# Sparse attention and a gated MLP on one core: rows of q and k of the local heads loaded as twelve tokens, with a new list for the first batch

## The chip, the cores and the metric

The kernel runs on one core of a Trainium2 chip. The metric is the device time of one execution in microseconds (us), as the median of several runs.

## The reference

Eight batches of 576 tokens go through an attention of eight heads of 64 columns, whose first four heads see a window of 32 tokens (local) and whose last four see every 32nd earlier token (strided). The result, with the heads side by side, goes through a gated MLP with a spatial gate.

```python
scores = (q @ k.T) / sqrt(64)             # per batch and head, 576 x 576
local   = (rel >= 0) & (rel < 32)         # heads 0 to 3, rel = row - column
strided = (rel >= 0) & (rel % 32 == 0)    # heads 4 to 7
x = softmax(masked scores) @ v            # 576 x 512 per batch
h = gelu_tanh(x @ w_in)                   # 512 -> 1024, halves u and v
v_s = w_sg @ (layernorm(v) * g_ln) + b_sg[:, None]
out = x + (u * v_s) @ w_out
```

## The kernel before

Work is tiled by batch. A pair of heads `hh` (0 and 1 are local, 2 and 3 strided) fills 128 partitions. For each pair q and k must stand turned, with the columns of a head on partitions and tokens along the row (`qT`, `kT`). In batch 0 and for the first part of batch 1 TensorE does this: `row_load` (`LR`) brings rows of q and k, `row_turn` (`RQ`, `RK`) multiplies them with an identity into PSUM (`tqq`, `tqk`), and `row_copy` (`CQ`, `CK`) copies them out into `qT` and `kT`. From the scores (`SL` into `sa` and `sr`, `SS` into `ss`) come masks, maximum, exponent, sum and product (`MK MX SB EX SU ML`, tiles `sml` for local and `sms` for strided heads), the turned probabilities (`PL`, `PS` into `ptl`, `pts`, copied out by `CL`, `CS`), and the product with v (`VA`, `VX`, `VY` into `ol`; `PV`, `PW` into `os`). That is x, turned; it is split in a high and a low part (`XH`, `XL` into `xt`), turned once more (`XR` into `xs`) and sent to DRAM (`XD`, four DMAs from ScalarE's queue). The MLP follows: `va` to `vd` (the v half of w_in, tile `v`), `u`, the gate `s` (tile `sg`, product `gt`) and `o`.

w_in and w_out are split into two parts in the first batch's time, in 16 pieces: `cl` loads, `ca` and the alternative form of `cb` run on ScalarE (ACT), `cb`, `cc` and `cd` on VectorE (DVE), `cg` on ACT, `ch` on GpSimd (POOL) or DVE; the tiles are `stage`, `cv`, `wih` and `wil`, `cs` and `cx` for w_out. The first matmul of `v` needs pieces 0 and 1.

Nothing is scheduled by a compiler. Three lists of words are written out by hand: `START` (all of batch 0's attention, the weights, and the front part of batch 1), `CYCLE` for batches 1 to 6 and `LAST`. `emit` runs a list word by word, and each engine keeps that order, so all instructions are recorded at one line (L81) and are told apart by tile names. A word's `@n` names one of four PSUM slots, `^` takes the other engine, `-` means the batch itself and no sign the next one. SP's queue issues the loads, also in the list's order. PE runs in list order too, and a matmul that must wait holds all behind it.

For local pairs `row9_load` and `row9_turn` (from line 458) put 9 tokens of one head on each of 128 partitions and turn each token's 64x64 block by itself, 18 matmuls per tensor, each recorded as two passes; one copy of 128x576 reads the slot out. For strided pairs `row_load` and `row_turn` put 12 tokens on each of 96 partitions and turn two tokens at a time, six transposes per tensor.

Of the kernel before, what the change touches and what calls it, by code (L numbers as in the profile page):

```python
# [22 lines left out]


START = """
ml= LR-:0 RK-@1:0 LZ-:0 LR-:1 RK-@2:1 cl=:3 cb=:3 TZ-:0 CK^-:0 cl=:1 ca=:1 cb=:1 ca=:3 cc=:3 RQ-@0:0
LR-:2 TZ-:1 cd=:3 RQ-@3:1 cl=:0 CK-:1 CQ^-:1 CQ-:0 SL-@0:0 MK-:4 ca=:0 MX-:4 mk= SL-@3:1 cb^=:0
LR-:3 cc=:1 wl=:1 MK-:5 MX-:5 SB-:4 EX-:4 SB-:5 RK-@2:2 RQ-@1:2 SU-:4 CQ-:2 RK-@0:3 CK-:2 ML-:4
RQ-@3:3 CK-:3 cc=:0 EX-:5 CQ-:3 TZ:0 mp=@1 cl=:9 ca=:9 LZ-:1 SU-:5 SS-@0:2 cl=:2 SS-@3:3 PL-@1:4
CL-:4 ML-:5 cd^=:1 cg=:1 MK-:2 PL-@21:5 CL-:5 cg=:3 MK-:3 wt=@0:1 MX-:3 LR:0 CM^-:5 wb= wh=:1 TZ:1  # L30
LV-:1 VA-@2:1 LR:1 cl=:4 cd=:0 LV-:0 cg=:0 ch=:1 MX-:2 XR-:1 wm=:1 SB-:3 EX-:3 SU-:3 RK@3:1 wc=
cb=:2 CK^:1 ca=:2 cl=:5 ca=:4 RK@0:0 CK^:0 SB-:2 EX-:2 VY-@1:0 XH-:1 XL-:1 cb=:9 cl=:6 XD-:1 VX-:0
LV-:3 wd= SU-:2 we= XHa-:0 cb^=:4 ML-:3 PS-@0:3 CS-:3 cl=:8 ch=:3 RQ@3:0 ca=:6 cc=:9 XR-:0 RQ@2:1
ch^=:0 ML-:2 LV-:2 CQ^:1 CQ:0 XD-:0 PS-@3:2 cc=:4 CS-:2 cb^=:8 PV-@2:3 PW-:3 XLa-:0 va@0:0 cb^=:5
cc=:2 PV-@3:2 PW-:2 cd^=:2 cl=:11 ca=:5 vb:0 cd=:4 cb^=:6 wl=:0 XHb-:0 cc=:6 lg= XH-:2 cg=:2 ca=:8
XLb-:0 cd=:6 XL-:2 ch=:2 XR-:2 XH-:3 XL-:3 SL@1:0 cg=:6 SL@3:1 cd=:9 cg=:9 ch=:9 MK:0 vc:0 cg=:4
cl=:7 cb=:7 ca=:7 MX:0 vd:0 g:0 wt=@1:0 wh=:0 ch=:4 cc=:5 cc=:8 cc=:7 wo= wp= cd=:5 LQ:3 cd=:8 LR:2
cd=:7 wm=:0 va@3:1 XD-:2 wl=:2 vb:1 vc:1 vd:1 cg=:5 XR-:3 cl=:13 g:1 cg=:7 ch=:6 xt cl=:10 LZ:1
cg=:8 v@0:2 vh TQ:3 RK@1:2 ls:1 CK:2 vl ls:0 RQ@2:2 CQ:2 LZ:0 lm:0 wl=:4 XD-:3 g:2 ls:2 ch=:5 ch=:7
u@3:1 ug:1 lm:1 lr:2 wt=@1:2 wh=:2 cb^=:11 wm=:2 SB:0 EX:0 SU:0 u@0:0 ca=:11 ug:0 LV:0 lm:2 wl=:3  # L40
cc=:11 LV:1 ML:0 cb=:10 u@2:2 wt=@0:4 wh=:4 wm=:4 SS@3:2 MK:2 u@1:3 PL@23:0 ca=:13 ug:2 lh:0 ll:0
lh:1 ll:1 ug:3 TZ+:1 cd=:11 CL:0 wt=@0:3 wh=:3 lh:2 cl=:15 wm=:3 ll:2 MX:2 cb=:13 ca=:10 cc=:10
TZ+:0 LQ+:0 cc=:13 SS@1:3 MK:3 s@2:0 sm:0 CM^:0 VA@3:1 XR:1 SB:2 EX:2 ca=:15 cd=:10 sh:0 sl^:0 TQ+:0
cg=:10 XH:1 ch=:8 s@0:1 cl=:12 MX:3 s@2:2 LQ+:1 XD:1 SB:3 EX:3 sm:1 sh:1 SU:2 cl=:14 cd=:13 ML:2
SU:3 ML:3 XL:1 cg=:11 ch^=:11 LV:2 sm:2 sh:2 sl:2 cb^=:12 cb^=:15 s@1:3 PS@2:3 PS@3:2 ch=:10 LQ+:3
sm:3 ca=:12 sl^:1 o@0:0 o:1 cg=:13 CS:2 PV@2:2 PW:2 CS:3 cc=:15 ch=:13 ca=:14 cd=:15 cg=:15 cb=:14
cc=:14 cd^=:14 cg=:14 cc=:12 cd^=:12 cg=:12 r VA@1:0 XH:0 ch=:12 sh:3 XR:2 XD:2 mr= ch^=:14 XL:0
XH:2 ch^=:15 o@3:2 o:3 sl^:3 o2:3 LV:3 XR:0 TQ+:1 os:3 od:3 o2:2 os:2 o2:1 LQ+:2 PV@3:3 LZ+:0 PW:3
rt o2:0 XR:3 os:0 od:0 LZ+:1 XH:3 XD:0 XD:3 od:2 LV+:1 os:1 od:1 XL:2 LV+:0 XL:3
"""  # L50
# [1089 lines left out]
```

## Time and profile before

| what | value |
|---|---|
| median of 3 runs | 556.45 us (555.75 to 558.96) |
| the profiled execution, its own time | 557.88 us |
| its span, first to last instruction | 556.2 us |
| mean granted TensorE clock | 0.975 |
| busy: PE, DVE, ACT, POOL | 534.1, 395.0, 224.7, 114.3 us |
| PE share of the span | 96% |

The span is what the trace covers, and the own time has 1.7 us around it. Busy times are means over a first batch in which PE often waits and seven batches in which it hardly does.

### The profile page before, as it was taken

To read this page: it belongs to the slowest core of one execution; us is meant where nothing else is said; L and a number is where in the kernel's file an instruction comes from. 1 tells how busy PE (TensorE), PEld (TensorE's weight loads), DVE (VectorE), ACT (ScalarE), POOL (GpSimd) and SP (SyncE) were. 2 spreads that over 40 slices of the span, in tenths; PEclk is the share of its full clock that TensorE was granted. 3 is DMA by queue.
4 is the path that set the end of the run, shared out by engine and by line. 5 is a ranking of instruction groups with operands and counts; after the bars stand their busy time and mean duration, and the time that the engine had idled before them with its cause. 6 is when DMAs were issued, how large, how long until landed. Compare 5 with 4: busy or idle time off the path is not lost.

```text
span 556.2 us, 17621 instructions
## 1 busy us (share of the span) xinstructions
PE 534.1 (96%) x7667; PEld 477.4 (86%) x7667; DVE 395.0 (71%) x686; ACT 224.7 (40%) x349; POOL 114.3 (21%) x164
## 2 busy tenths in 40 slices
PE   5769999999999999999999999999999999999997
PEld 5668888888998899888998899888997889978995
DVE  1796999977956788668956779568957689454622
ACT  2474685405531255315531064415532055413420
POOL 4361713511041010301031010301031010400030
PEclk9576999999999999999999999999999999999999
DMA  8998596879717685279617585189716670045002
GB/s 233 239 233 188 143 160 107 166 155 179 156 18 175 135 126 133 38 178 166 150 17 176 98 155 139 28 181 159 156 27 143 123 173 0 30 116 146 2 1 94
DMA packets 248847, 70.12 MB, mean 126 GB/s; under 512 B 232897, under 2 KB 232897, under 8 KB 248770
## 3 DMA queue, kind: packets, MB, share of 16 engines
q1 hardware_dynamic: 167746, 50.11, 43.6%
q10 hardware_dynamic: 81024, 18.89, 16.1%
q8 instruction: 60, 0.98, 0.8%
q14 instruction: 17, 0.14, 0.1%
HBM read 50.09 MB, written 18.87 MB: 124 GB/s over the span
## 4 chain that ended last, share of the span: by engine, by line
PE 89%; DVE 4%; DMA 3%; issue 2%; ACT 1%; SPq 0%; DVEq 0%; ACTq 0%
PE v L81 19%; PE sg L81 19%; PE u L81 18%; PE o L81 17%; PE ol L81 3%; PE os L81 3%; PE sa L81 2%; PE ss L81 2%; DMA stage<-in_moe_w_in_dram 2%; PE pts L81 1%; PE tqq L81 1%; PE tqk L81 1%; PE ptl L81 1%; DMA out_dram<-ob 1%; DVE wol L81 1%
## 5 line engine op out<-in xcount | busy, mean ns | idle before, releaser
L81 PE MATMUL sg<-wsh,vg 128*128 128x288 f32 x512 | 107.9, 296 | 0.1
L81 PE MATMUL u<-xt,wih 128*128 128x288 f32 x512 | 102.4, 295 | 0.0
L81 PE MATMUL o<-woh,vg 128*128 128x512 f32 x288 | 95.0, 397 | 0.6 <-ACT pts L81 0.6
L81 PE MATMUL v<-wih,xt 128*128 128x512 f32 x256 | 84.6, 400 | 0.0
L81 PEld LDWEIGHTS sg<-wsh,vg 128*128 128x128 f32 x512 | 83.6, 188 | 0.9 <-ACT ptl L81 0.3
L81 PEld LDWEIGHTS u<-xt,wih 128*128 128x128 f32 x512 | 82.3, 188 | 0.9 <-issue 0.3
L81 PE MATMUL sg<-wsl,vg 128*128 128x288 f32 x256 | 75.5, 295 | 0.3 <-DVE wsl L81 0.3
L81 PE MATMUL u<-xt,wil 128*128 128x288 f32 x256 | 75.5, 295 | 0.0
L81 PEld LDWEIGHTS o<-woh,vg 128*128 128x128 f32 x288 | 54.1, 188 | 13.1 <-ACT pts L81 1.7
L81 ACT ACT_TABLE_LOAD x30 | 38.5, 1283 | 55.4 <-DMA xd<-xs 21.2
L81 DVE TENSOR_TENSOR gt<-sg,u 128x576 f32<-128x576 f32 x32 | 23.6, 753 | 51.8 <-PE sg L81 37.8
L81 PEld LDWEIGHTS v<-wih,xt 128*128 128x128 f32 x256 | 48.6, 190 | 10.9
L81 PE MATMUL o<-wol,vg 128*128 128x512 f32 x144 | 56.2, 390 | 0.0
L81 PE MATMUL v<-wil,xt 128*128 128x512 f32 x128 | 50.4, 394 | 0.0
L81 POOL TENSOR_TENSOR vg<-gt,vg 128x576 fp32r<-128x576 f32 (+2 forms) x36 | 35.6, 1012 | 71.5 <-ACT vg L81 71.5
L81 PEld LDWEIGHTS sg<-wsl,vg 128*128 128x128 f32 x256 | 48.0, 188 | 0.6 <-DVE wsl L81 0.6
L81 PEld LDWEIGHTS u<-xt,wil 128*128 128x128 f32 x256 | 48.0, 188 | 0.0
L81 DVE TENSOR_TENSOR ob<-o,xn 128x512 f32<-128x512 f32 x32 | 21.6, 677 | 28.2 <-PE o L81 28.1
L81 POOL TENSOR_TENSOR sms<-sms,mx 100x576 f32<-100x576 f32 x10 | 12.5, 1258 | 140.4 <-DVE mx L81 140.3
L81 DVE BATCH_NORM_STATS2 bnst<-hv 128x6 f32<-128x512 f32 (+1 forms) x40 | 26.9, 672 | 13.5 <-ACT hv L81 13.5
L81 ACT CAST vg<-gt 128x576 fp32r<-128x576 f32 (+2 forms) x48 | 22.3, 512 | 32.3 <-DVE gt L81 32.3
L81 ACT COPY pts<-pts 100x576 f32<-100x576 f32 x16 | 10.1, 638 | 54.2 <-PE pts L81 27.5
(140 smaller groups left out, 922.7 us busy)
## 6 DMA issues: line engine op xcount, KB each, us to landing
xd<-xs ACTq DMA_DIRECT2D x128, 72.0 KB
xn<-xd SPq DMA_DIRECT2D x8, 1024.0 KB
out_dram<-ob ACTq DMA_DIRECT2D x32, 256.0 KB
rawq<-in_q_dram SPq DMA_DIRECT2D x100, 72.0 KB
rawk<-in_k_dram SPq DMA_DIRECT2D x100, 72.0 KB
v<-in_v_dram SPq DMA_DIRECT2D x16, 288.0 KB
...
```

Of the source, the lines that this page charges most:

```text
L81: ins = self.tc.keep_in_program_order(op(*args, **kwargs))
```

## The change

`row9_load` and `row9_turn` go. All four pairs take the form with 12 tokens on 96 partitions and six transposes. For a local pair the tokens of a head then stand in the wrong half of the partitions for every second token, so `row_copy` reads a slot out in four quarters of 64 partitions x 288; two of them read from one half of the partitions and write into the other. It concerns eight tensors (q and k of two local pairs, batches 0 and 1): PE's passes for them go from 288 to 48, the copies from 8 to 32. `START` is written anew throughout, the loads' order included; `CYCLE` and `LAST` stay.

```diff
--- before.py
+++ after.py
@@ -23,30 +23,30 @@
 START = """
-ml= LR-:0 RK-@1:0 LZ-:0 LR-:1 RK-@2:1 cl=:3 cb=:3 TZ-:0 CK^-:0 cl=:1 ca=:1 cb=:1 ca=:3 cc=:3 RQ-@0:0
-LR-:2 TZ-:1 cd=:3 RQ-@3:1 cl=:0 CK-:1 CQ^-:1 CQ-:0 SL-@0:0 MK-:4 ca=:0 MX-:4 mk= SL-@3:1 cb^=:0
-LR-:3 cc=:1 wl=:1 MK-:5 MX-:5 SB-:4 EX-:4 SB-:5 RK-@2:2 RQ-@1:2 SU-:4 CQ-:2 RK-@0:3 CK-:2 ML-:4
-RQ-@3:3 CK-:3 cc=:0 EX-:5 CQ-:3 TZ:0 mp=@1 cl=:9 ca=:9 LZ-:1 SU-:5 SS-@0:2 cl=:2 SS-@3:3 PL-@1:4
-CL-:4 ML-:5 cd^=:1 cg=:1 MK-:2 PL-@21:5 CL-:5 cg=:3 MK-:3 wt=@0:1 MX-:3 LR:0 CM^-:5 wb= wh=:1 TZ:1
-LV-:1 VA-@2:1 LR:1 cl=:4 cd=:0 LV-:0 cg=:0 ch=:1 MX-:2 XR-:1 wm=:1 SB-:3 EX-:3 SU-:3 RK@3:1 wc=
-cb=:2 CK^:1 ca=:2 cl=:5 ca=:4 RK@0:0 CK^:0 SB-:2 EX-:2 VY-@1:0 XH-:1 XL-:1 cb=:9 cl=:6 XD-:1 VX-:0
-LV-:3 wd= SU-:2 we= XHa-:0 cb^=:4 ML-:3 PS-@0:3 CS-:3 cl=:8 ch=:3 RQ@3:0 ca=:6 cc=:9 XR-:0 RQ@2:1
-ch^=:0 ML-:2 LV-:2 CQ^:1 CQ:0 XD-:0 PS-@3:2 cc=:4 CS-:2 cb^=:8 PV-@2:3 PW-:3 XLa-:0 va@0:0 cb^=:5
...
+LR-:0 RQ-@2:0 RK-@0:0 cl=:1 LR-:1 RQ-@1:1 ca=:1 LR-:2 CQ^-:0 TZ-:0 CQ-:1 CK^-:0 cl=:3 ml= SL-@0:0
+MK-:4 MX-:4 SB^-:4 ca=:3 cb^=:1 cb^=:3 TZ-:1 cc=:1 cl=:0 RK-@2:1 LZ-:1 CK-:1 ca=:0 cb=:0 cd^=:1
+cc=:3 cd^=:3 cg=:3 SL-@1:1 MK-:5 MX-:5 RK-@2:2 CK-:2 LZ-:0 wl=:1 EX-:4 LR-:3 RK-@1:3 cc=:0 SU-:4
+RQ-@0:2 wb= mk= mp=@2 CK-:3 cl=:9 LV-:1 CQ-:2 SS-@0:2 MK-:2 SB-:5 RQ-@1:3 CQ^-:3 cg=:1 SS-@1:3 LV-:0
+TZ:1 LR:0 wc= ML-:4 EX-:5 PL-@3:4 CL-:4 wt=@2:1 wh=:1 SU-:5 ML-:5 PL-@30:5 MK-:3 MX-:3 MX-:2 wm=:1
+CL-:5 CM-:5 VA-@2:1 SB-:3 EX-:3 SU-:3 SB-:2 EX-:2 TZ:0 wd= cd^=:0 ML-:3 cl=:2 ca=:2 cb^=:2 LR:1
+ca=:9 XH-:1 RK@1:0 RQ@1:0 CK:0 XL-:1 XR-:1 XD-:1 ch=:3 cl=:4 RK@0:1 we= CK:1 VY-@3:0 ca=:4 SU-:2
+VX-:0 RQ@1:1 cb=:4 cl=:6 ca=:6 XHa-:0 CQ^:0 cl=:8 ca=:8 cc=:2 cd^=:2 PS-@0:3 CQ:1 cc=:4 LV-:3 ML^-:2
+cg=:0 cl=:5 PS-@1:2 XLa-:0 CS-:3 ch=:1 PV-@2:3 PW-:3 XR-:0 ch^=:0 cb=:6 cc=:6 cb=:8 CS-:2 cc=:8
+cd=:8 XD-:0 cb=:9 LV-:2 cd=:4 cd=:6 cg=:4 cc=:9 va@0:0 vb:0 cb=:5 cg=:2 wl=:0 PV-@3:2 PW-:2 cl=:7
...
@@ -453,42 +453,8 @@
     ROWS = S // RT
     HOMES = ("wsh", "wsl", "wol", "woh")
 
-    ROWS9 = S // 9
-
-    def row9_load(b, hh):
-
-        if b == 0:
-            both = p1.tile([P, 2, 9 * D], F32, tag=HOMES[hh], name=f"rows_{b}_{hh}")
-        for n, (nm, src) in enumerate((("q", q), ("k", k))):
-            if b == 0:
-                raw = both[:, n]
-            else:
-                raw = p1.tile([P, 9 * D], F32, tag="raw", name=f"rows{nm}_{b}_{hh}", bufs=4)
-            sp.dma_start(
-                raw, src[b, 2 * hh : 2 * hh + 2].rearrange("h (p j) d -> (h p) (j d)", j=9)
-            )
-            state[b, hh, "raw" + nm] = raw
-
-    def row9_turn(b, hh, nm):
-
-        raw = state[b, hh, "raw" + nm]
-        ps = psum(f"tq{nm}_{b}_{hh}").rearrange("p a c -> p (a c)")
-        state[b, hh, "rows"] = True
-        state[b, hh, "turn" + nm] = ps[:, 0:S].rearrange("p (j m) -> p m j", m=ROWS9)
-        for j in range(9):
-            for hp in range(2):
-                r = slice(ROWS9 * hp, ROWS9 * hp + ROWS9)
-                pe.matmul(
-                    ps[64 * hp : 64 * hp + 64, j * ROWS9 : j * ROWS9 + ROWS9],
-                    raw[r, j * D : j * D + D], ident[r, r],
-                    start=True, stop=True,
-                )
-
     def row_load(b, hh):
 
-        if hh < NH // 2:
-            row9_load(b, hh)
-            return
         if b == 0:
             both = p1.tile([P, 2, 2 * RT * D], F32, tag=HOMES[hh], name=f"rows_{b}_{hh}")
         for n, (nm, src) in enumerate((("q", q), ("k", k))):
@@ -504,13 +470,10 @@
 
     def row_turn(b, hh, nm):
 
-        if hh < NH // 2:
-            row9_turn(b, hh, nm)
-            return
         raw = state[b, hh, "raw" + nm]
         ps = psum(f"tq{nm}_{b}_{hh}")
         state[b, hh, "rows"] = True
-        state[b, hh, "turn" + nm] = ps[:, :, 0:SH].rearrange("p a (c m) -> p m a c", m=ROWS)
+        state[b, hh, "turn" + nm] = ps[:, :, 0:SH]
         for j in range(RT):
             half, col = divmod(j, RT // 2)
             pe.transpose(
@@ -527,13 +490,22 @@
             state[b, hh, nm] = p2.tile([P, S + ST], F32, tag=nm + "T", name=f"{nm}T_{b}_{hh}")
             dst = state[b, hh, nm][:, 0:S]
         if hh < NH // 2:
-            to = dst.rearrange("p (m j) -> p m j", j=9)
+            to = dst.rearrange("p (m a c t) -> p t m a c", a=2, c=RT // 2, t=2)
+            of = src.rearrange("p a (c h m) -> p h m a c", h=2, m=ROWS // 2)
+            parts = [
+                (to[64 * h : 64 * h + 64, t], of[64 * t : 64 * t + 64, h])
+                for h in range(2) for t in range(2)
+            ]
         else:
-            to = dst.rearrange("p (m a c) -> p m a c", a=2, c=RT // 2)
-        if alt[0]:
-            dve.tensor_copy(to, src)
-        else:
-            act.copy(to, src)
+            parts = [(
+                dst.rearrange("p (m a c) -> p m a c", a=2, c=RT // 2),
+                src.rearrange("p a (c m) -> p m a c", m=ROWS),
+            )]
+        for to, of in parts:
+            if alt[0]:
+                dve.tensor_copy(to, of)
+            else:
+                act.copy(to, of)
 
     def k_zeros(b, hh):
 
```

PE at the start of the program (`tqq`, `tqk` are turned rows, `sa` and `sr` local scores). Before:

```order
L81 MATMUL tqk_0_124<-ident,rows_0_121 64x64 x18
L81 MATMUL tqk_1_148<-ident,rows_1_145 64x64 x18
L81 MATMUL tqq_0_179<-ident,rows_0_121 64x64 x18
L81 MATMUL tqq_1_204<-ident,rows_1_145 64x64 x18
L81 MATMUL sa_229<-kT_0_169,qT_0_227 32x64 x36
L81 MATMUL sa_229<-kT_1_201,qT_1_225 32x64 x22
L81 MATMUL sr_285<-kT_1_201,qT_1_225 32x64 x2
L81 MATMUL sa_229<-kT_1_201,qT_1_225 32x64 x6
L81 MATMUL sr_285<-kT_1_201,qT_1_225 32x64 x6
```

The same place on PE in the changed kernel:

```order
L81 MATMUL tqq_0_96<-ident,rows_0_93 128x96 x6
L81 MATMUL tqk_0_103<-ident,rows_0_93 128x96 x6
L81 MATMUL tqq_1_114<-ident,rows_1_111 128x96 x6
L81 MATMUL sa_171<-kT_0_131,qT_0_126 32x64 x36
L81 MATMUL tqk_1_221<-ident,rows_1_111 128x96 x6
L81 MATMUL sa_171<-kT_1_217,qT_1_133 32x64 x22
L81 MATMUL sr_241<-kT_1_217,qT_1_133 32x64 x2
L81 MATMUL sa_171<-kT_1_217,qT_1_133 32x64 x6
L81 MATMUL sr_241<-kT_1_217,qT_1_133 32x64 x6
```

The first scores now stand between the third and the fourth turned tensor, and the rows come q first.

ACT, the part that turns batch 1's local rows while batch 0's probabilities `pts` are copied out. Before:

```order
L81 ACTIVATE sms_90<-sms_90 100x16x36
L81 CAST xt<-ol_1_525 128x2x9x32
L81 DMA xd_645<-xs_1_576 32x18x32 x4
L81 CAST wst<-bst 32x576
L81 CAST xt<-ol_0_636 128x2x8x32
L81 ACTIVATE stage<-stage 128x512
L81 COPY pts_3_711<-pts_3_694 100x576
L81 ACTIVATE cv_735<-stage 128x512
L81 COPY qT_0_766<-tqq_0_716 128x576
L81 DMA xd_645<-xs_0_738 32x18x32 x4
L81 COPY pts_2_790<-pts_2_772 100x576
```

On ACT, from the split of `ol_1` to the copy of `pts_3`, in the changed kernel:

```order
L81 ACTIVATE cx<-cs_338 128x256
L81 CAST xt<-ol_1_494 128x2x9x32
L81 COPY kT_0_539<-tqk_0_555 64x288 x4
L81 DMA xd_576<-xs_1_574 32x18x32 x4
L81 COPY kT_1_429<-tqk_1_583 64x288 x4
L81 ACTIVATE cv_600<-stage 128x512
L81 ACTIVATE cv_647<-stage 128x512
L81 CAST xt<-ol_0_595 128x2x8x32
L81 ACTIVATE cx<-cs_655 128x256
L81 COPY qT_1_677<-tqq_1_638 64x288 x4
L81 CAST wih<-cv_234 128x512
L81 COPY pts_3_707<-pts_3_660 100x576
```

Three sets of quarters for batch 1 now stand on ACT ahead of the copy of `pts_3`, with four DMA issues between the first two; before, no copy for batch 1 stood ahead of it.

DVE, the same part. Before:

```order
L81 TENSOR_SCALAR stage<-stage 128x512
L81 COPY kT_1_519<-tqk_1_587 128x576
L81 COPY kT_0_379<-tqk_0_614 128x576
L81 TENSOR_TENSOR xt<-ol_1_525,xt 128x2x9x32
L81 TENSOR_SCALAR cs_384<-cs_384 128x256
L81 TENSOR_REDUCE sr_2_686<-sms_90 100x16
```

On DVE, from the sums of `sms_90` on, in the changed kernel:

```order
L81 TENSOR_REDUCE sr_2_602<-sms_90 100x16
L81 TENSOR_SCALAR sr_2_602<-sr_2_602 100x16
L81 RECIPROCAL sr_2_602<-sr_2_602 100x16
L81 TENSOR_SCALAR stage<-stage 128x512
L81 COPY qT_0_650<-tqq_0_562 64x288 x4
L81 SCALAR_TENSOR_TENSOR cv_545<-cv_545,stage 128x512
L81 SCALAR_TENSOR_TENSOR cv_545<-stage,cv_545 128x512
L81 SCALAR_TENSOR_TENSOR cv_600<-cv_600,stage 128x512
L81 TENSOR_TENSOR sms_90<-sms_90,sr_2_602 100x16x36
L81 TENSOR_TENSOR xt<-ol_0_595,xt 128x2x8x32
```

Of batch 1's local copies DVE keeps `qT_0` alone, and takes the product on `sms_90` from POOL.

## Rows read from the trace of the kernel before

**Rows 1.** The chain of waits that ended last: start us, us, what.

```profile
38.16 4.12 issue
```

**Rows 2.** Stretches: window, length, busy us (instructions) of PE, PEld, DVE, ACT, POOL; PEclk, DMA, GB/s.

```profile
5.00:10.00 5.00, 3.66 (x68) 3.47 (x67) 0.00 (x0) 0.00 (x0) 2.82 (x11) 1.00 0.94 283
10.00:15.00 5.00, 3.53 (x79) 3.39 (x76) 2.09 (x4) 1.83 (x4) 0.00 (x0) 1.00 1.04 227
...
42.30:50.00 7.70, 7.68 (x130) 6.78 (x130) 4.57 (x8) 3.42 (x7) 0.00 (x0) 0.50 0.83 196
50.00:80.00 30.00, 30.00 (x444) 25.97 (x443) 27.86 (x55) 21.98 (x39) 13.70 (x15) 1.00 0.81 157
```

**Rows 3.** Timeline of PE: start us, us, operation, count [idle before, releaser].

```profile
18.67 0.77 PE L81 MATMUL sa<-kT,qT 64*32 64x64 f32 x35 [0.62 <-issue]
...
20.11 1.22 PE L81 MATMUL tqk<-ident,rows 96*128 96x96 f32 x6
21.13 1.16 PE L81 MATMUL tqq<-ident,rows 96*128 96x96 f32 x6
...
24.71 2.54 PE L81 MATMUL ss<-kT,qT 64*36 64x36 f32 x128
...
42.28 2.61 PE L81 MATMUL tqq<-ident,rowsq 64*64 64x64 f32 x44 [4.12 <-issue]
...
45.75 1.94 PE L81 MATMUL os<-pts,v 36*64 36x36 f32 x64
47.62 0.79 PE L81 MATMUL v<-wih,xt 128*128 128x512 f32 x1
...
51.44 0.50 PE L81 MATMUL v<-wih,xt 128*128 128x512 f32 x1
...
53.03 1.42 PE L81 MATMUL sa<-kT,qT 64*32 64x64 f32 x116
```

**Rows 4.** Waits of PE from 47.6 us on: us in total, times, longest.

```profile
PE ptl L81 <- DVE sms L81: 1.2, 1, 1.2
PE pts L81 <- DVE gt L81: 0.9, 1, 0.9
```

**Rows 5.** Groups of PE up to 50 us, by form: count, busy us, mean ns, idle before.

```profile
L81 PE MATMUL tqq<-ident,rowsq 64*64 64x64 f32 x72 | 3.6, 278 | 4.1 <-issue 4.1
...
L81 PE MATMUL tqk<-ident,rows 96*128 96x96 f32 x12 | 2.4, 369 | 0.0
```

**Rows 6.** DMA of 39 to 41 us: queue, packets, MB, share of 16 engines.

```profile
q8 instruction: 1, 0.02, 2.9%
```

**Rows 7.** Timeline of ACT: start us, us, operation, count [idle before, releaser].

```profile
13.16 1.24 ACT L81 ACTIVATE cv<-stage 128x512 f32<-128x512 f32 x2 [8.84 <-DMA stage<-in_moe_w_in_dram]
...
14.83 0.62 ACT L81 COPY qT<-tqq 128x576 f32<-128x576 f32 x1
17.98 0.67 ACT L81 ACTIVATE cv<-stage 128x512 f32<-128x512 f32 x1 [2.53 <-DMA stage<-in_moe_w_in_dram]
...
46.09 0.64 ACT L81 COPY pts<-pts 100x576 f32<-100x576 f32 x1 [2.43 <-DMA xd<-xs]
...
52.64 0.44 ACT L81 ACTIVATE cx<-cs 128x256 f32<-128x256 f32 x1
52.97 0.63 ACT L81 CAST xt<-os 128x576 fp32r<-128x576 f32 x1
...
62.22 0.62 ACT L81 CAST wih<-cv 128x512 fp32r<-128x512 f32 x1 [1.43 <-DMA xd<-xs]
```

**Rows 8.** Timeline of DVE, same columns.

```profile
10.88 0.43 DVE L81 TENSOR_SCALAR stage<-stage 128x512 int32<-128x512 int32 x1 [10.88 <-DMA stage<-in_moe_w_in_dram]
...
26.66 3.07 DVE L81 TENSOR_TENSOR sms<-ss,mask_s 36x576 f32<-36x576 f32 x4
...
44.94 0.76 DVE L81 COPY qT<-tqq 128x576 f32<-128x576 f32 x1 [3.11 <-PE tqq L81]
```

**Rows 9.** Page, costliest groups: count, busy us, mean ns, idle before.

```profile
L81 POOL TENSOR_TENSOR sms<-sms,mx 100x576 f32<-100x576 f32 x10 | 12.5, 1258 | 140.4 <-DVE mx L81 140.3
```

More of the change, by code (lines that the diff above doesn't have):

```diff
@@ L31 @@
-LV-:1 VA-@2:1 LR:1 cl=:4 cd=:0 LV-:0 cg=:0 ch=:1 MX-:2 XR-:1 wm=:1 SB-:3 EX-:3 SU-:3 RK@3:1 wc=
-cb=:2 CK^:1 ca=:2 cl=:5 ca=:4 RK@0:0 CK^:0 SB-:2 EX-:2 VY-@1:0 XH-:1 XL-:1 cb=:9 cl=:6 XD-:1 VX-:0
-LV-:3 wd= SU-:2 we= XHa-:0 cb^=:4 ML-:3 PS-@0:3 CS-:3 cl=:8 ch=:3 RQ@3:0 ca=:6 cc=:9 XR-:0 RQ@2:1
-ch^=:0 ML-:2 LV-:2 CQ^:1 CQ:0 XD-:0 PS-@3:2 cc=:4 CS-:2 cb^=:8 PV-@2:3 PW-:3 XLa-:0 va@0:0 cb^=:5
-cc=:2 PV-@3:2 PW-:2 cd^=:2 cl=:11 ca=:5 vb:0 cd=:4 cb^=:6 wl=:0 XHb-:0 cc=:6 lg= XH-:2 cg=:2 ca=:8
-XLb-:0 cd=:6 XL-:2 ch=:2 XR-:2 XH-:3 XL-:3 SL@1:0 cg=:6 SL@3:1 cd=:9 cg=:9 ch=:9 MK:0 vc:0 cg=:4
@@ L37 @@
[L37 to L48, printed above, removed]
@@ L49 @@
-rt o2:0 XR:3 os:0 od:0 LZ+:1 XH:3 XD:0 XD:3 od:2 LV+:1 os:1 od:1 XL:2 LV+:0 XL:3
+LR-:0 RQ-@2:0 RK-@0:0 cl=:1 LR-:1 RQ-@1:1 ca=:1 LR-:2 CQ^-:0 TZ-:0 CQ-:1 CK^-:0 cl=:3 ml= SL-@0:0
[3 more added lines that the diff above has]
+TZ:1 LR:0 wc= ML-:4 EX-:5 PL-@3:4 CL-:4 wt=@2:1 wh=:1 SU-:5 ML-:5 PL-@30:5 MK-:3 MX-:3 MX-:2 wm=:1
@@ new lines @@
+CL-:5 CM-:5 VA-@2:1 SB-:3 EX-:3 SU-:3 SB-:2 EX-:2 TZ:0 wd= cd^=:0 ML-:3 cl=:2 ca=:2 cb^=:2 LR:1
[3 more added lines that the diff above has]
+cd=:8 XD-:0 cb=:9 LV-:2 cd=:4 cd=:6 cg=:4 cc=:9 va@0:0 vb:0 cb=:5 cg=:2 wl=:0 PV-@3:2 PW-:2 cl=:7
+ch=:2 ch=:4 cd^=:9 cg=:9 ch=:9 SL@1:0 XHb-:0 XLb-:0 SL@3:1 XR-:2 cl=:11 cb=:11 XH-:2 XH-:3 XL-:2
@@ new lines @@
+vc:0 cb=:7 ca=:7 cc=:7 ca=:5 cc=:5 XL-:3 vd:0 g:0 LR:2 xt MK:0 LQ:3 cd^=:7 cg=:7 ch=:7 LZ:1 wo=
+va@1:1 vb:1 cg=:6 MX:0 XD-:2 ch=:6 wt=@0:0 TQ:3 cl=:13 lg= wh=:0 wm=:0 vc:1 vd:1 g:1 cd=:5 wp= cg=:5
+ch=:5 wl=:2 cl=:10 v@0:2 ls:1 XR-:3 ca=:11 RK@3:2 CK:2 u@1:1 vh XD-:3 vl g:2 cl=:15 ls:0 lm:0
+wt=@2:2 wh=:2 ls:2 wm=:2 SB:0 EX:0 ug:1 RQ@3:2 u@0:0 ug:0 lm:1 lr:2 u@2:2 CQ:2 SU:0 lh:1 SS@3:2
+cc=:11 ug:2 lm:2 ll:1 ML:0 wl=:4 LV:1 wt=@1:4 wh=:4 MK:2 u@2:3 SS@0:3 PL@21:0 wm=:4 MX:2 wl=:3 LZ:0
+LV:0 lh:2 lh:0 ll:0 ug:3 cb^=:13 ll:2 wt=@3:3 CL:0 ca=:13 cc=:13 wh=:3 wm=:3 TZ+:1 LQ+:0 SB:2 LQ+:1
@@ new lines @@
+EX:2 cd^=:11 cg=:11 MK:3 ch^=:11 cb=:10 MX:3 s@2:0 CM^:0 cd^=:13 ca=:10 VA@3:1 s@0:1 LV:2 sm:0 sh:0
+cc=:10 cd^=:10 cb=:15 cg=:13 XR:1 cg=:10 ca=:15 cc=:15 XH:1 cl=:14 XD:1 SB:3 TZ+:0 TQ+:0 sl^:0
+cl=:12 sm:1 sh:1 SU:2 XL:1 ch=:10 cg=:8 sl^:1 EX:3 SU:3 s@1:2 cb=:14 sm:2 ML^:2 s@0:3 sm:3 LQ+:3
+ca=:12 ML:3 PS@2:3 cb^=:12 sh:2 ch=:13 rt VA@3:0 PS@1:2 CS:3 ca=:14 ch^=:8 cc=:12 o@0:0 o:1 LV:3
+cc=:14 o@2:2 cd=:12 XH:0 sl:2 cd=:14 CS:2 PV@1:2 PW:2 cg=:12 cd=:15 cg=:15 o:3 TQ+:1 ch^=:15 sh:3
+mr= ch=:12 XR:2 r XL:0 cg=:14 ch^=:14 sl^:3 o2:2 XR:0 o2:3 os:3 XD:2 os:2 od:2 LQ+:2 LZ+:0 XH:2
@@ L50 @@
+PV@3:3 PW:3 XH:3 XL:2 o2:1 o2:0 os:1 XR:3 XL:3 os:0 XD:3 XD:0 LZ+:1 od:0 LV+:1 od:1 od:3 LV+:0
 """
```

## The prediction

> **What bounds the kernel now.** I read the chain of waits that ended last first. Nearly all of it is PE's own matmuls; the one long piece of it that is neither work nor the first loads is 4.12 us at 38.16 us, an idle PE with nothing to wait for [rows 1]. The stretches come next: from 50 to 80 us PE is busy for all 30.00 us, so from the first `v` matmul on PE sets the end, and a change in the first 50 us is worth what it moves that start [rows 2]. In the timeline of PE that start is at 47.62 us, right behind `os`, and the 4.12 us stand ahead of batch 1's last turned rows [rows 3]. Not all of a shift at 47.62 us reaches the end: later PE waits 1.2 us and 0.9 us for DVE, and a PE that comes later waits less there [rows 4]. The working below is a walk from the loads to `os`. Its sum is made against the profiled execution's own 557.88 us, which is 1.43 us above the median of 556.45 us. About 0.5%, or 2.8 us, is what a measurement here can tell from no change: faster is below 553.7 us, slower above 559.2 us.
>
> **Passes.** 240 of 288 passes on PE go. 72 old passes (two tensors) took 3.6 us, 12 new ones (two tensors) 2.4 us [rows 5], and start to start six new ones take 1.0 us [rows 3]. Batch 1's four tensors so cost 4 us in place of 7. Batch 0's lie in waits for loads, where they are worth nothing as such.
>
> **The idle 4.12 us.** It ends with no event of another engine; within 39 to 41 us one packet of 0.02 MB for instructions landed on queue q8 [rows 6]. I read it as PE waiting for its own instructions, after long runs of passes of a few tens of ns each. With 240 fewer in front of it, it most likely goes. [...]
>
> What is late next, once the stall is gone, is ACT. So I walk through its new order.
>
> **Loads.** `cl3` is now the eighth load, 2752 KB through its end by the tile sizes. Before, 1664 KB had landed at 10.88 [rows 8], 2176 KB at 13.16 and 3264 KB at 17.98 us [rows 7], and between the last two 2752 KB falls at 15.7. All six row loads before it now have 96 rows in place of 128. The stretch with 128-row loads moved 283 GB/s, the next 227 [rows 2], so a load of 288 KB could take 1.30 in place of 1.04 us, and four more of this kind are 1.0 us. I take the middle, 16.2 (15.7 to 16.7).
>
> **A quarter copy.** The trace has no copy of 64 x 288, and none from one half of the partitions to the other. From below: 256 columns on ACT go by in 0.33 us, start to start (52.64 to 52.97); from above: a whole copy of 576 takes 0.62 [rows 7]. 288 columns are nearest to the first: I take 0.35, so 1.4 us for a set of four, against 0.6 for the copy that it replaces.
>
> **The walk.** ACT operations over 512 or 576 columns are 0.6 us [rows 7], DVE's 0.75 [rows 8].
> - `cl3` 16.2; ACT does one `cv`, two stage tails and the set of `kT_1`, 0.6 + 1.2 + 1.4: 19.4. Then the second local scores, 1.4 (before: 18.67 to 20.11 [rows 3]): 20.8. So nothing is won in the first 20 us, though the first scores come sooner.
> - `tqk_2`, `tqk_3`, `tqq_2`: 3 x 1.0, 23.8. ACT's copy of `qT_2` 0.6, `ss_2` half of 2.54 us [rows 3]: 25.7. DVE: two masks of 0.77 [rows 8] and `qT_3` 0.8: 28.0. `ss_3` 1.3: 29.3. Both `ss` ended at 27.2 before.
> - DVE masks `sms_91` 1.5 and takes its maximum: 31.5. POOL subtracts in `sms_91` and `sms_90`, 1.26 each [rows 9]: 34.1. ACT's exponent of the second: 34.7.
> - ACT then has `wst`, `cv`, a tail, `cx` and the high part of `ol_1`, 4 x 0.6 + 0.3: 37.4. Set `kT_0`: 38.8. Four DMA issues of `xd`: ACT stood still 2.43 and 1.43 us at two such sets [rows 7]; the middle, 1.9: 40.7. Set `kT_1`: 42.1. Two `cv`, the high part of `ol_0`, `cx`, 2.1: 44.2. Set `qT_1`: 45.6. `wih` and the copy of `pts_3`, 1.2: 46.8.
> - `os_3` 1.9 [rows 3]: **`v` starts at 48.7**, against 47.62: 1.1 later. DVE's own set, `qT_0`, ends near 42 and its product on `sms_90` near 44, hidden under ACT's work; were ACT 3 us shorter they would be next. SP brings batch 1's rows behind two sets of v loads now; I cost that at nothing, since `tqk_0` isn't wanted before 37.4 us, and what they came later than that would be late in full. POOL has two products fewer.
>
> **The clock.** [...] Six `v` matmuls took 2.75 us at the lower level and six 1.59 us at the upper (51.44 to 53.03) [rows 3]. The new list puts twelve of them ahead of `os_2`, behind a PE that waits for ACT much of the time. If the clock again rises about 8 us after steady work resumes (here `os_3` at 46.8), all twelve run at the lower level: 1.2 us more. PE is then 2.3 us behind.
>
> **What is absorbed.** Between batch 1's first local mask and its third `gt`, the new DVE order has two `cv` words (0.7 each), a stage tail and one small `cx` fewer, some 1.9 us. DVE then comes no later than before, and the 2.1 us that PE waited for it [rows 4] can swallow nearly all of the lag: 0.2 is left. If DVE gains nothing, 2.3 are left. I take 1.0. **Sum:** 557.88 + 1.0 = 558.9 for such an execution, and 556.45 + 1.0 = **557.5 for the median**.
>
> **Rivals.**
> - *Faster: ACT keeps up.* `cl3` at 15.7 (0.5), DMA issues that run beside copies (1.9), POOL's two subtractions beside other work (1.3) and quarters at 0.33 take some 4 us from the walk: `v` starts near 44.5, the stall's 4.12 us and the passes are won. 3.2 us earlier than before, with DVE's 1.9 us to keep it: 553.3. For it: the engine's queue runs ahead of its work elsewhere. Against it: 2.43 us is what such an issue cost at just this place.
> - *Slower: quarters cost as much as whole copies.* If reading across partition halves or the short rows make one quarter 0.6 us, the four sets on ACT are 4 x 4 x 0.27 = 4.3 us longer, all on the walk. The lag is 6.6, less 2.1 absorbed: 4.5, 560.9. It turns the sign from about 0.5 us a quarter on. Against it: the 256-column rows.
> - *Loads of 96 rows take a third longer.* Their 288 KB then need 1.39 in place of 1.04 us, 1.4 us by `cl3`, 0.9 more than the walk has: 558.4. Against it: 512 KB without such loads took 2.28 us (10.88 to 13.16) and 1088 KB with two of them 4.82, the same 225 KB a us. [...]
> - *The stall comes back behind `v`'s start.* The 64 passes of `os`, 72 records of scores and 128 of `ss` are still there. 4.1 us once more, less 2.1 absorbed: 560.8. That the change does less than it says is part of this: the passes go, the stall stays.
>
> **How the numbers follow.** Forecast 0.45, with a range of its own of 555 to 560; ACT keeps up 0.24; quarters dear 0.15; loads slower 0.08; stall again 0.08. Faster: 0.22 of the first rival and 0.03 of the forecast, 0.25. Slower: 0.13, 0.03 and 0.07 of the others and 0.05 of the forecast, 0.28. The rest, 0.47, is within 0.5%. The range goes from a little below the first rival, 552.8, to a little above the second, 561.3.
>
> **What would show it.** Right: no idle piece of some us put down to "issue" on PE before `v`; ACT busy without a gap from about 35 to 47 us; PE ahead of `os_3` waiting for ACT's copy of `pts_3`; first `v` at 48 to 49.5; quarters of 0.3 to 0.45; waits of PE for DVE behind 50 us well under 2.1. Wrong: a first `v` before 46, quarters over 0.5 us, `cl3` outside 15 to 17, or an "issue" idle of several us behind `v`'s start. Behind 104 us nothing should differ by more than some tenths.

## The result, and the profile after

The changed kernel takes 561.64 us (median of 8 runs, 560.18 to 563.29), the kernel before 555.84 us in its 8 runs of the same comparison (555.14 to 558.96). The ratio is 1.0089, 95% interval 1.0062 to 1.0116: slower by 3.4 to 6.4 us, clear of noise. The forecast was 557.5 with "within 0.5%" as the likeliest class; the time lies 0.3 us above the range's upper end, and in the class "slower", which had 0.28. Beside three experiments the unchanged copy of the changed kernel came out at 1.0083 (1.0057 to 1.0110).

The profiled executions differ by less, 561.47 against 557.88 us, since that of before lies 2 us above the median of its runs and that of after on it. So the traces have 3.6 us to explain.

The chain that ended last, after: two of the quarter copies on it, the first `v`, and the first scores of `CYCLE` (start, us, what). A word in small letters means the batch itself, so `CYCLE`'s first pass does the MLP of batch 1 and the scores of batch 2.

```profile
36.05 0.42 ACT kT L81
...
40.45 0.42 ACT kT L81
...
48.42 5.11 PE v L81 x12
...
125.47 1.30 PE sa L81 x82
```

The same chain of before, two runs of turning passes on it, and the same scores:

```profile
31.75 2.63 PE tqk L81 x60
...
42.28 2.61 PE tqq L81 x44
...
121.73 1.31 PE sa L81 x84
```

The 4.12 us of [rows 1] are not in this trace; the longest piece of the chain put down to "issue" ahead of the first `v` is 0.39 us now (39.63). But `CYCLE`'s first scores come 3.74 us later (125.47 against 121.73); from there on both kernels run the same lists, and the span ends 3.6 us later (559.8 against 556.2). So all of it is made in `START`. The path to the first `v` has changed: before, the passes that turn batch 1's local rows lay on it and none of their copies; now three sets of quarter copies on ACT do, and none of the passes. PE after (start, us, operation, count, idle before and releaser), which answers to [rows 3]:

```profile
31.57 1.72 PE L81 MATMUL ol<-ptl,v 64*64 64x32 f32 x56 [1.86 <-issue]
...
37.37 1.22 PE L81 MATMUL tqq<-ident,rowsq 96*128 96x96 f32 x6 [2.50 <-ACT kT L81]
...
45.17 0.90 PE L81 MATMUL pts<-ident,sms 36*100 36x36 f32 x16 [1.56 <-ACT qT L81]
46.48 1.94 PE L81 MATMUL os<-pts,v 36*64 36x36 f32 x64 [0.40 <-ACT pts L81]
48.35 0.79 PE L81 MATMUL v<-wih,xt 128*128 128x512 f32 x1
...
53.46 1.14 PE L81 MATMUL os<-pts,v 36*64 36x36 f32 x64
54.53 1.41 PE L81 MATMUL sa<-kT,qT 64*32 64x64 f32 x116
57.06 0.25 PE L81 MATMUL sr<-kT,qT 64*32 64x64 f32 x2 [1.12 <-DVE xt L81]
...
57.56 0.50 PE L81 MATMUL v<-wih,xt 128*128 128x512 f32 x1
```

The first `v` starts at 48.35 (47.62 before), so 0.7 us late; the first `sa` behind it at 54.53 (53.03), 1.5 late; the second half of `v` at 57.56. ACT, which answers to [rows 7]:

```profile
13.41 0.66 ACT L81 ACTIVATE cv<-stage 128x512 f32<-128x512 f32 x1 [1.11 <-DMA stage<-in_moe_w_in_dram]
...
35.63 1.68 ACT L81 COPY kT<-tqk 64x288 f32<-64x288 f32 x4
37.24 2.05 ACTq L81 DMA_DIRECT2D xd<-xs  x4
39.58 1.72 ACT L81 COPY kT<-tqk 64x288 f32<-64x288 f32 x4 [2.27 <-DMA xd<-xs]
...
43.45 1.67 ACT L81 COPY qT<-tqq 64x288 f32<-64x288 f32 x4
...
45.78 0.64 ACT L81 COPY pts<-pts 100x576 f32<-100x576 f32 x1
```

ACT is busy from 34 to 46.4 us but for 2.27 us at the four DMA issues, and `os` waits for its copy of `pts`. A quarter takes 0.42 us, a set 1.7. DVE:

```profile
31.20 0.27 DVE L81 TENSOR_TENSOR wst<-wsgT,wsh 64x128 fp32r<-64x128 f32 x1
...
39.45 1.85 DVE L81 COPY qT<-tqq 64x288 f32<-64x288 f32 x4
```

A set on DVE takes 1.85. The 1.86 us at 31.57 that the timeline of PE puts down to "issue" are DVE's: `ol` takes the PSUM slot that the first of these rows (`wst`, until 31.47) still reads, and every trace of the new list has the piece there, 1.85 to 1.89 us long. PE's waits from 46 to 127.2 us (total, times, longest), which answer to [rows 4]:

```profile
PE sr L81 <- DVE xt L81: 1.1, 1, 1.1
PE sg L81 <- ACT ptl L81: 0.9, 1, 0.9
PE sg L81 <- DVE wsl L81: 0.8, 1, 0.8
PE u L81 <- POOL wil L81: 0.7, 1, 0.7
PE ptl L81 <- ACT u L81: 0.5, 1, 0.5
PE os L81 <- ACT pts L81: 0.4, 1, 0.4
```

That is 4.4 us, where before had 2.4 in this stretch. Neither of the two waits that were to shrink is there; five new ones are, and the one of `sg` for `wsl` has grown from 0.3 to 0.8.

The granted clock after, in the stretches around the first `v` (length, PE's busy time and instructions, PEclk, DMA, GB/s):

```profile
46.00:50.00 4.00, 3.60 (x70) 0.50 0.87 205
50.00:52.00 2.00, 2.00 (x6) 0.50 0.57 145
52.00:54.00 2.00, 2.00 (x41) 0.74 0.72 221
54.00:56.00 2.00, 1.94 (x159) 1.00 1.19 202
```

The same of before:

```profile
50.00:52.00 2.00, 2.00 (x68) 0.95 0.94 246
```

The upper level comes some 3 us later.

### The profile page after: what moved, and what is told of

Same layout as the page of the kernel before. It is cut to its first block, busy times and chain, and to the rows that moved or that the text cites. A ratio compares the mean times of both kernels' runs of the same rounds, so it can differ in the third digit from the quotient of the medians.

```text
span 559.8 us, 17173 instructions
## 1 busy us (share of the span) xinstructions
PE 531.4 (95%) x7427; PEld 473.5 (85%) x7427; DVE 397.7 (71%) x702; ACT 229.8 (41%) x361; POOL 111.4 (20%) x160
## 3 DMA queue, kind: packets, MB, share of 16 engines
q10 hardware_dynamic: 81024, 18.89, 16.2%
HBM read 50.09 MB, written 18.87 MB: 123 GB/s over the span
## 4 chain that ended last, share of the span: by engine, by line
PE 89%; ACT 3%; DMA 2%; DVE 2%; SPq 1%; issue 1%; POOL 1%; ACTq 0%
PE sg L81 21%; PE v L81 19%; PE o L81 18%; PE u L81 18%; PE os L81 3%; PE ol L81 3%; PE ss L81 2%; PE sa L81 2%; DMA stage<-in_moe_w_in_dram 2%; PE pts L81 1%; SPq L81 1%; ACT kT L81 1%; PE ptl L81 1%; DVE sms L81 1%; PE sr L81 0%
## 5 line engine op out<-in xcount | busy, mean ns | idle before, releaser
L81 POOL TENSOR_TENSOR vg<-gt,vg 128x576 fp32r<-128x576 f32 (+2 forms) x36 | 35.7, 1013 | 74.6 <-ACT vg L81 74.1
```

The lines of the kernel that those rows point to most:

```text
L81: ins = self.tc.keep_in_program_order(op(*args, **kwargs))
```

## The experiments

**Form and list apart.** Two kernels take one half of the change each. e1, against the changed kernel (the list is that of before throughout):

```diff
-LR-:0 RQ-@2:0 RK-@0:0 cl=:1 LR-:1 RQ-@1:1 ca=:1 LR-:2 CQ^-:0 TZ-:0 CQ-:1 CK^-:0 cl=:3 ml= SL-@0:0
+ml= LR-:0 RK-@1:0 LZ-:0 LR-:1 RK-@2:1 cl=:3 cb=:3 TZ-:0 CK^-:0 cl=:1 ca=:1 cb=:1 ca=:3 cc=:3 RQ-@0:0
...
```

e2, against it (the three functions are those of before):

```diff
+        if hh < NH // 2:
+            row9_load(b, hh)
+            return
...
-            to = dst.rearrange("p (m a c t) -> p t m a c", a=2, c=RT // 2, t=2)
+            to = dst.rearrange("p (m j) -> p m j", j=9)
...
```

> The list of before with the twelve-token form and the quarter copies. Theory (the new list loses the time, not the form): 240 passes are gone, and with them the idle 4.12 us; against that six quarter sets on DVE and ACT take 1.1 us more each, partly under other work. First v matmul at 44 to 47 us, median 552 to 556 us, faster than before or the same. Rival (the form loses it: quarter copies of 0.42 us and loads of 96 rows): first v at 48 or later, median 559 us or more.

> The new list with nine tokens on 128 rows, 64x64 passes and one copy per tensor, as before. Theory (the list loses it): still slower than before, 559 to 564 us; each copy on ACT is 1.1 us shorter but 240 passes are back, and PE waits for ACT and DVE in the same places; first v at 47 to 50 us. Rival (the form loses it): 557 us or less, first v at 46 or earlier.

e1: 1.0038 (1.0004 to 1.0072), 559.71 against 556.79 us. e2: 1.0046 (1.0009 to 1.0083), 559.04. By their middles each half costs about half of the loss, and together they make the 1.0089. Both theories put it all on the list: in e1 the rival came out instead (first `v` behind 48, above 559 us), in e2 the theory, at its lower edge. So neither half alone is to blame. In e1 the first `v` came at 49.97, 2.4 us later than before, and from there to `CYCLE`'s first scores all took as long as before. Its PE still stood idle with nothing to wait for that the trace shows, 2.00 us, now in another place, between the transposes of one tile of `w_sg`:

```profile
29.35 0.46 PE L81 MATMUL wsgT<-ident,wsg 64*128 64x64 f32 x8
31.81 0.24 PE L81 MATMUL wsgT<-ident,wsg 64*64 64x64 f32 x2 [2.00 <-issue]
```

So dropping 240 passes doesn't remove such an idle piece for certain. Where the form lost its time here DVE shows:

```profile
37.00 3.73 DVE L81 COPY kT<-tqk 64x288 f32<-64x288 f32 x8
...
46.15 1.85 DVE L81 COPY qT<-tqq 64x288 f32<-64x288 f32 x4
```

The eight quarters lie on e1's chain, 3.6 us where two whole copies take 1.5. The other set ends at 48.00, and `os`, which takes the slot that it reads, starts at 48.10; the 2.43 us that the profile puts down to "issue" ahead of `os` are this set (before, the one copy ended at 45.70 [rows 8] and `os` started at 45.75). In e2 the first `v` came at 46.85, sooner than before, but `sr` waited 1.51 us, 1.02 us ahead of `sa` were put down to "issue", the granted clock fell once more (0.63 and 0.51 from 56 to 60 us), and `CYCLE`'s first scores came at 126.0.

**What the quarters cost.** e5 reads each local tensor out in two copies over all 128 partitions. It leaves out the crossing of the halves, so only its time is of use.

```diff
-            parts = [
-                (to[64 * h : 64 * h + 64, t], of[64 * t : 64 * t + 64, h])
-                for h in range(2) for t in range(2)
-            ]
+            parts = [(to[:, t], of[:, t]) for t in range(2)]
```

> The changed kernel with each local tensor read out by two copies of 128 x 288 in place of four of 64 x 288; nothing crosses the partition halves, so tokens of the local heads stand in wrong places. It halves the copy time and keeps all else. Theory (the form's cost is its copies: four sets of 1.7 us on ACT and two of 1.87 us on DVE stand on the way to the first v): a set takes 0.85 to 0.95 us, the first v comes 2 to 3.5 us before that of the changed kernel run beside it, and 1.5 to 3 us of the time come back. Rival (the copies lie under other waits): the time within 1 us of the changed kernel.

1.0028 (1.0003 to 1.0054), 558.13 against the 560.83 of e8 beside it: 2.7 us back. Its ACT and its PE:

```profile
41.70 0.73 ACT L81 COPY qT<-tqq 128x288 f32<-128x288 f32 x2
```

```profile
45.53 0.79 PE L81 MATMUL v<-wih,xt 128*128 128x512 f32 x1
```

Two copies take 0.72 us where four took 1.70, and the first `v` is at 45.53, against 49.18 in e8. The theory held: the copy sets stand in the way of the first `v`. Its sets were a little shorter than expected (0.85 to 0.95) and the first `v` 3.65 us sooner, not 2 to 3.5.

**A third form.** e10 (list of before) and e11 (new list) load six tokens of both heads per row, turn each token of each head by itself into its own half of the partitions, and read out with one copy.

```diff
+                    heads.rearrange("h (p j) d -> p h (j d)", j=RT),
...
+                    pe.matmul(
+                        ps[64 * hp : 64 * hp + 64, half, col * ROWS : col * ROWS + ROWS],
+                        raw[:, (hp * RT + j) * D : (hp * RT + j + 1) * D], ident[0:ROWS, 0:ROWS],
```

> The list of before with a third form: 96 rows hold six tokens of both heads, each token of each head is turned by a matmul of 96 x 64 into its own half of the partitions (12 matmuls, 24 passes per tensor in place of 36), and one copy of 128 x 576 reads the slot out. 96 passes fewer than before, no copy more. Theory (passes and code are worth something, quarters cost): 0 to 4 us faster than before, first v at 43.5 to 47.6. Rival (the idle PE put down to instructions comes back in another place, and loads of 96 rows in 1536-byte pieces are slower): as before or up to 3 us slower.

> The same third form with the new list. Theory (the quarters cost the form's share of the loss, the list the rest): copies on ACT and DVE are 0.64 and 0.75 us again, first v 2 to 4 us sooner than in the changed kernel, 557 to 560 us, that is 0.1 to 0.5% over before. Rival (the quarters were not what cost): within 1 us of the changed kernel.

e10: 1.0041 (1.0007 to 1.0074); its profiled execution was a short one (span 554.0), but its runs scatter from 554.99 to 563.09, and its trace has 2.77 us of "issue" in the middle of a set of scores. e11: 1.0097 (1.0067 to 1.0127), no gain over the changed kernel, against the theory; its first `v` came at 49.93, later than the changed kernel's 48.35. Its PE:

```profile
34.21 0.31 PE L81 MATMUL ol<-ptl,v 64*64 64x32 f32 x1 [2.41 <-issue]
...
37.96 2.19 PE L81 MATMUL tqq<-ident,rowsq 96*64 96x96 f32 x24 [0.79 <-ACT kT L81]
39.94 2.13 PE L81 MATMUL tqk<-ident,rowsk 96*64 96x96 f32 x24
```

One tensor's 24 passes take 2.0 us start to start (37.96 to 39.94), where six took 1.0. In e11 the copies are short again, and the chain runs through the passes of all four tensors and an idle 2.41 us in the middle of `ol`. A tensor's passes and its copies take 1.0 and 1.7 us in the changed kernel, 1.8 and 0.62 before [rows 5, 7], 2.0 and 0.64 in e11, 1.0 and 0.72 in e5. They are not to be added up as they stand, since only a part of each lies on the path: in e11 the passes and the idle piece, in the changed kernel the copies. Without the 2.41 us e11's first `v` would come at some 47.5 (an estimate from these rows), about where it was before; so it is not shown that the third form itself loses.

**What follows the first `v`.** e3 puts `os_2` between the two sixes of `v`, as before; e4 splits `os_2` before it is turned.

```diff
-cd=:8 XD-:0 cb=:9 LV-:2 cd=:4 cd=:6 cg=:4 cc=:9 va@0:0 vb:0 cb=:5 cg=:2 wl=:0 PV-@3:2 PW-:2 cl=:7
+cd=:8 XD-:0 cb=:9 LV-:2 cd=:4 cd=:6 cg=:4 cc=:9 va@0:0 cb=:5 cg=:2 wl=:0 PV-@3:2 PW-:2 vb:0 cl=:7
```

```diff
-ch=:2 ch=:4 cd^=:9 cg=:9 ch=:9 SL@1:0 XHb-:0 XLb-:0 SL@3:1 XR-:2 cl=:11 cb=:11 XH-:2 XH-:3 XL-:2
+ch=:2 ch=:4 cd^=:9 cg=:9 ch=:9 SL@1:0 XHb-:0 XLb-:0 SL@3:1 cl=:11 cb=:11 XH-:2 XH-:3 XL-:2 XR-:2
```

> The changed kernel with os_2 behind the first six v matmuls, as in the list of before, in place of behind twelve. Theory (a lag of 1.2 us comes from twelve matmuls at the lower clock, and 1.1 us of PE waiting at sr comes from os_2 being late for its readers): the wait at sr shrinks to 0 to 0.3 us, the second half of v starts 1 to 1.5 us earlier than 57.56, and 1 to 2 us of the time come back (559.5 to 560.5). Rival (later waits for ACT, DVE and POOL set the end anyway): within 0.5 us of the changed kernel.

> The changed kernel with one word moved: the turning of os_2 into xs comes behind its split in high and low part, as before, so that ACT's read of os_2 does not wait for DVE's. Theory: ACT's split starts 0.8 us earlier, the 1.12 us of waiting at sr go, 0.5 to 1.1 us of the time come back. Rival (absorbed later): no difference, within 0.4 us.

e3: 1.0090 (1.0051 to 1.0128), e4: 1.0082 (1.0045 to 1.0119). With intervals of 2 us either way these times can't tell the theories from the rival, but the traces can: what was to come back did not. In e3 the wait at `sr` was gone, but `os_2` now waited 0.67 us for DVE's split of `ol_0`, whose slot it takes. Its matmuls also stayed slow for longer, and the second half of `v` came at 60.31:

```profile
57.69 2.03 PE L81 MATMUL sa<-kT,qT 64*32 64x64 f32 x115
```

These scores took 1.41 us in the changed kernel, and e3's `os_2` 1.94 in place of 1.14, as long as `os_3` took in the changed kernel (46.48) at a granted clock of 0.50. (e3's profile gives the granted clock as 1.00 throughout; the matmuls' own times contradict it.) In e4 ACT's split starts right behind `os_2`, and `sr` still waited 0.99 us, now for the turning: `sr` takes `os_2`'s slot, whose three readers (ACT's 0.6 us, DVE's 0.76 and 0.77) run one behind the other in either order.

**ACT ahead of the first `v`.** e6, e9 and e12 move the copy of `pts_3` and `wih` ahead of the set of `qT_1`, and turn `pts_2` behind six `v`; they differ in where the DMA issues stand.

```diff
...
-PS-@0:3 CQ:1 cc=:4 LV-:3 ML^-:2
-cg=:0 cl=:5 PS-@1:2 XLa-:0 CS-:3 ch=:1 PV-@2:3 PW-:3 XR-:0 ch^=:0 cb=:6 cc=:6 cb=:8 CS-:2 cc=:8
+PS-@0:3 CS-:3 cg=:0 CQ:1 cc=:4 LV-:3 ML^-:2
+cl=:5 PV-@2:3 PW-:3 XLa-:0 ch=:1 XR-:0 ch^=:0 va@0:0 XHb-:0 XLb-:0 XD-:0 PS-@1:2 cb=:6 cc=:6 cb=:8 CS-:2 cc=:8
...
```

(This is e12; e6 has both `XD` behind `CS-:2` and `XHb` behind them, e9 `XD-:1` behind `cg=:0` and `XD-:0` behind `CS-:2`. e12 also splits `os_2` before it is turned, as e4 does.)

> The changed kernel with ACT's order changed ahead of the first v: the four DMA issues of ol_1's rows come behind the copy of pts_2, the copy of pts_3 and the wih that v needs come ahead of the set of qT_1, and pts_2 is turned between the first and second six v matmuls. Theory (ACT's order sets the first v): the first v at 45 to 46.5, 2 to 3 us sooner; of this 1 to 3 us reach the end, 558 to 560. Rival (what follows the first v, the readers of os_2 and later waits, sets the end): the first v sooner, but the time within 1 us of the changed kernel.

> The ACT order of e6_pts_first mended: ol_1's four DMA issues stand behind the copy of pts_3 and ahead of the set of qT_1, and the last 64 columns of ol_0 are split ahead of the second four issues, not behind them. Theory (where ACT's DMA issues stand cost e6 its 10 us): first v 2 to 3 us sooner than in the changed kernel, os_2 waits under 1 us, the time 1 to 3 us under the changed kernel. Rival (any delay of the weights' conversion on ACT costs the same): os_2 or the second half of v waits again, the time as in the changed kernel or above.

> As e9_act_order, but ol_1's four DMA issues stay where the changed kernel has them, ol_0's stand ahead of the copy of pts_2, and os_2 is split before it is turned. Theory (e9's 3.88 us at sr came from late sends, which hold SP's loads of v_2 and the buffer of xs_2, not from the copies' order): first v near 46.2 us as in e9, v_2 loaded in time, the wait at sr 1.2 us or less, the second half of v 1 to 2.5 us sooner than 57.6, 558 to 560 us. Rival (the new list's loss lies behind the first v whatever ACT does): sr waits 2 us or more again, or the time stays at 561 and above.

In all three the first `v` came where it was expected, 45.5, 46.4 and 46.5, and in none did the time come back: 1.0254 (1.0218 to 1.0290), 1.0168 (1.0144 to 1.0192) and 1.0102 (1.0054 to 1.0149). In e6 eight DMA issues in one piece held ACT, with the last 64 columns of `ol_0` behind them (ACT's queue), and `os_2`, which takes `ol_0`'s slot, waited 5.37 us:

```profile
48.89 4.93 ACTq L81 DMA_DIRECT2D xd<-xs  x8
53.86 1.14 ACT L81 CAST wih<-cv 128x512 fp32r<-128x512 f32 x2 [4.39 <-DMA v<-in_v_dram]
...
55.21 0.20 ACT L81 CAST xt<-ol 128x64 fp32r<-128x64 f32 x1
```

In e9 ol_1's sends went out later, and with them SP's loads of `v_2` (49.57, SP's queue; 41.99 in e12) and the turning of `os_2` (57.15, DVE); `sr` waited 3.88 us. In e12, which mends these and turns `os_2` later, `sr` waited 0.36, and yet:

```profile
44.66 1.94 PE L81 MATMUL os<-pts,v 36*64 36x36 f32 x64 [0.74 <-ACT pts L81]
46.52 0.79 PE L81 MATMUL v<-wih,xt 128*128 128x512 f32 x1
...
53.08 1.94 PE L81 MATMUL os<-pts,v 36*64 36x36 f32 x64
54.95 2.04 PE L81 MATMUL sa<-kT,qT 64*32 64x64 f32 x116
57.34 0.32 PE L81 MATMUL sr<-kT,qT 64*32 64x64 f32 x2 [0.36 <-DVE xs L81]
...
58.17 0.61 PE L81 MATMUL v<-wih,xt 128*128 128x512 f32 x1
```

The first `v` is 1.8 us sooner than in the changed kernel, the second half 0.6 later (58.17). Every piece between takes longer: `os` 1.94 us against 1.14 at 53.46 in the changed kernel, `sa` 2.04 against 1.41. The clock of e12:

```profile
50.00:52.00 2.00, 2.00 (x12) 0.50 0.31 50
...
54.00:56.00 2.00, 2.00 (x114) 0.50 1.17 225
...
58.00:60.00 2.00, 2.00 (x14) 0.89 0.51 70
```

It stays at the lower level to about 58 us. What PE did before was much the same in both, with 0.74 us of idle time ahead of `os` here; why the level rose 5 us later here was not settled. In e9, whose PE goes through the same list and the same 0.74 us up to there, the second six `v` already ran at the upper level from 49.75 on (0.39 us for a `wil` matmul, against 0.63 in e12). So e12's trace doesn't show what its order of ACT is worth with the clock of the others.

**The first set on ACT.** e7 moves the set of `kT_1` for batch 0 ahead of the words that wait for `cl3`.

```diff
-MK-:4 MX-:4 SB^-:4 ca=:3 cb^=:1 cb^=:3 TZ-:1 cc=:1 cl=:0 RK-@2:1 LZ-:1 CK-:1 ca=:0
+TZ-:1 RK-@2:1 CK-:1 MK-:4 MX-:4 SB^-:4 ca=:3 cb^=:1 cb^=:3 cc=:1 cl=:0 LZ-:1 ca=:0
```

> The changed kernel with the set of kT_1 for batch 0 ahead of the weight words that wait for the second load of w_in on ACT. Theory (the walk on ACT and DVE hands a gain on): the second local scores start 2 to 3 us sooner than at 16.1, the strided scores 1 to 2 us, the first v 0.5 to 1.5 us. Rival (the conversion of weights, now later, is what v waits for, or other waits fill in): the first v not sooner, the time within 1 us.

> The changed kernel once more, beside these three: 0.6 to 1.2% slower than before.

1.0085 (1.0058 to 1.0112) against e8's 1.0083 (1.0057 to 1.0110). The second scores came at 14.40, 2.6 us sooner than in e8, and two tensors later PE waited for rows instead; the first `v` was no sooner (49.75 against 49.18):

```profile
20.89 1.19 PE L81 MATMUL tqk<-ident,rows 96*128 96x96 f32 x6 [2.91 <-DMA rows<-in_k_dram]
```

No version here beats the kernel before.

## Why the prediction was right and wrong

**Right: the walk's end.** The first `v` was forecast at 48.7 and came at 48.35, with ACT the engine that sets it and `os_3` waiting for the copy of `pts_3`, as said. Step by step:

| milestone, us | forecast | measured |
|---|---|---|
| `cl3` landed | 16.2 | 13.4 |
| second local scores done | 20.8 | 18.5 |
| both `ss` done | 29.3 | 27.5 |
| high part of `ol_1` done | 37.4 | 35.7 |
| set `kT_0` done | 38.8 | 37.3 |
| DMA issues past | 40.7 | 39.6 |
| set `kT_1` done | 42.1 | 41.3 |
| set `qT_1` done | 45.6 | 45.1 |
| first `v` | 48.7 | 48.35 |

That it came within 0.35 us is in part luck: two sizes were off and partly made up for each other, the loads 2.8 us early and each set 1.7 us, not 1.4. The wait of 2.27 us at the DMA issues (forecast 1.9) was there. No run shows a load of 96 rows that takes a third longer: `cl3`, behind six of them, landed 2.8 us ahead of the walk, as far as loads that overlap can show it.

**Right: the clock term's kind, smaller.** The twelve `v` and `os_2` took 6.18 us from 48.35 to 54.53, where six, `os_2` and six took 5.41 before: 0.8 us, forecast 1.2. The two levels are the 0.50 and 1.00 of [rows 2]. The upper one came before the twelve were through (0.50 up to 52 us, 0.74 from 52 to 54, 1.00 from 54). In e12 it came some 5 us later behind much the same work (0.50 up to 58 us), so the step's guess of when it rises, taken from the one trace of before, does not carry over.

**Wrong: the step "What is absorbed".** It let 1.3 of 2.3 us of lag vanish in waits of PE for DVE. The lag was 1.5 at `sa`, less than said, and then it grew: 2.8 at the second half of `v` (57.56 against 54.75), 3.7 at `CYCLE`'s first scores. The two waits of [rows 4] did go, but the new list has waits of its own in their stead. The first is `sr` <- DVE, 1.1 us: `sa` and `sr` stand right behind `os_2`, and `sr` takes its slot, where before six `v` matmuls stood between. The others are `sg` for ACT and DVE, `u` for POOL's `wil` and `ptl` for ACT. The new order was on record, but the step counted DVE's work alone. That the list and not the form makes this part the halves show: from the first to the second half of `v` it takes 9.2 us in the changed kernel and 10.5 in e2, both with the new list, but 7.1 before and in e1; and from there to `CYCLE`'s first scores, 0.9 us more in the changed kernel than before, and in e1 as before. What the waits alone are worth isn't shown: in e3 and e12 the one at `sr` was gone or short, but in both the upper level also came later, which costs time of its own.

**Half right: "Passes".** PE's passes went as said, but e1 shows that the form alone loses 0.4% under the old list. The 3 us of passes that the step wins were on the path before, and the path then moved to the copies: in the changed kernel three sets on ACT and the DMA issues between them, in e1 three sets on DVE. The price of a set was in the walk, at 1.4 in place of 1.7; that the copies outweigh the passes under either list was not said.

**The rivals.** "ACT keeps up" failed on the sets and the issues. "Quarters cost as much as whole copies" was nearest: 0.42 us lies between the forecast 0.35 and its turning point of 0.5, and in e5 halving the sets brought 2.7 us back. Slower loads did not come. The stall did not come back ahead of `v` in the changed kernel, but did in e1, e10 and e11, so it is not shown that fewer passes took it away. Nor is it shown that the kernel before has it in every execution: only one trace of it exists, of an execution 2 us above the median. The trace of the changed kernel has such a piece of 1.44 us far behind, among `sr` matmuls of a list that both kernels run (380.38), where that of before has none. That PE waits for its own instructions in such pieces was the author's estimate: the traces have 2.0 to 4.1 us of it (e1, e10, e11, before) and name no releaser.

What stays open: the split of the new list's 0.46% between its waits and the clock, and some 2 us by which the medians differ more than the profiled executions. A stall that is shorter in most executions of the kernel before than in its trace would account for them; no run shows it.
